# Reordering the RMS chains of a streaming-attention and SwiGLU kernel on one core: block pairs, an order by hand on VectorE, and two copies that change their engine

## The chip, the cores and the metric

The kernel runs on one core of a Trainium2 chip. The metric is the time of one execution on the device, in microseconds (us). A core has several engines, each with its own instruction queue: TensorE (PE in the profile, its weight loads PEld), VectorE (DVE), ScalarE (ACT), GpSimd (POOL) and SyncE (SP, which here only issues DMAs). They meet at semaphores. Matmul results land in PSUM, here eight banks of 128 x 512 fp32; everything else lies in SBUF.

## What is computed

```python
# attention: q, k, v are (4, 8, 768, 64); n_sink 4, window 128
scores = scale * np.matmul(q, k.transpose(0, 1, 3, 2))
keep = is_sink | in_window          # keys 0..3, and the last 128 up to the query
scores = np.where(keep, scores, -1000000000.0)
a = softmax(scores)
attn = np.matmul(a, v)
# the heads side by side: x is (3072, 512)
rms = np.sqrt(np.mean(x * x, axis=-1, keepdims=True) + 1e-06)
xn = x / rms * rms_g
g = xn @ w_gate                     # 512 -> 1536
silu = g * (1.0 / (1.0 + np.exp(-g)))
out = (silu * (xn @ w_val)) @ w_out # 1536 -> 512
```

Inputs and output are fp32; the kernel works in bf16 with fp32 sums.

## The kernel before, in words

The 3072 tokens are 24 blocks of 128 (6 in each of 4 batches). Four blocks make a group of 512 tokens (`GB`, `GN`); there are 6 groups. The feed-forward of group G runs on TensorE while the attention of the blocks of group G+1 and G+2 is fitted in between.

*Attention of block g.* `unit_t`/`unit_t1` transpose q and k on TensorE into PSUM (`pqk`) and copy them out (`qkT`, L257, L279); from block 14 on, except at a batch's start, SP does it by DMA transposes. `unit_s` makes the scores (`pT`, L411), ScalarE their exponentials (`et`, L420), and `mask` zeroes what lies outside the window, on VectorE for the early blocks (L386), else on GpSimd (L388, L393). `unit_attend` multiplies with v: `unit_sink_av` (L444) opens two banks `pv`, `unit_av` (L458, L462) adds to them, VectorE divides by the sum (`rden` L494, `x` L499), and ScalarE squares with an accumulate (`sq`, L510).

*RMS chain.* `unit_rms(gs)` turns the sums of squares of the blocks in `gs` into reciprocal roots by seven small VectorE instructions (`m` L527 and `y` L533 to L555), a few columns wide, whatever the number of blocks. `unit_xr(g)` scales the block (L573, on VectorE; L569 for block 0, L567 on ScalarE for block 1). `unit_x(g)` transposes the result on TensorE (`pxt`, L596) and copies it to `xnt` (ScalarE L603). From block 12 on `unit_xr` issues an SP DMA transpose in place of all that. `GROUP` says which blocks share a chain: (0,1), (2,3), (4,5), (6), (7), then four at a time.

*Feed-forward.* `parts_f` gives a gate part and a value part per slice of 128 columns of the 1536: `pg` matmuls, ScalarE's tanh `th` (L636); `pvl` matmuls, VectorE's `p` (L641) and `hT` (L649). In groups 1 to 5 that makes 24 parts of four matmuls each. Group 0 is done in two halves of 256 tokens with two slices a part, `fa` then `fb`, 12 parts each. `parts_o` adds 12 output parts (`po` L664, three per block); ScalarE copies the result (`osb`, L671) and SP stores it.

*Order.* `run(parts, slots)` walks the parts; a slot (s, unit) is emitted ahead of part s. The lists of slots are: one for the first half, inline; `FIRST` for the second half and group 0's output; and for later groups what `step` gives, plus the RMS chain of the next group's four blocks: `unit_rms` at part 22, `unit_xr` at 25 and 26, `unit_x` at 27 to 30. For blocks 3, 5, 6 and 7 `unit_av` itself emits the chain. The program order is the engine's order on PE, SP and Pool (`MANUAL`). On VectorE and ScalarE the framework's scheduler orders the instructions, except in the prologue, up to `masks` (L746), where all engines follow the program (`MANUAL_ALL`).

*PSUM.* All accumulators share one pool of eight banks (tag `b1`). A new tile waits until the last reader of its bank is done; that reader is an engine's instruction some eight tiles back, so a late `hT` or `et` holds up a matmul that has nothing else to do with it.

*Weights.* `w_gate` and `w_val` come in six chunks each, `w_out` in two, on GpSimd's DMA queue between the loads of q, k and v, during the prologue and the first half.

Of the kernel before, what the change touches and what calls it, by code (L numbers as in the profile page):

```python
# [28 lines left out]
def kernel(  # L29
# [13 lines left out]
    nc = tc.nc  # L43
# [8 lines left out]
    NB = B * NT  # L52
# [120 lines left out]
    def unit_g():  # L173

        pt = psum.tile([P, 512], FP32, name="pgt", tag="b1")
        for kt in range(KTN):
            nc.tensor.matmul(
                out=pt[:, kt:kt + 1], lhsT=raw[2][0:1, kt * P:(kt + 1) * P],
                rhs=gb[0:1, 0:1], start=True, stop=True, skip_group_check=True,
            )  # L180
        ps = psum.tile([P, 512], FP32, name="pgb", tag="b1")
        nc.tensor.matmul(
            out=ps, lhsT=gb[0:1, 0:P], rhs=raw[2][0:1, :], start=True, stop=True,
        )
        nc.vector.tensor_copy(out=gb, in_=ps)
        nc.scalar.copy(out=gt, in_=pt[:, 0:KTN])

    def unit_cast(i):
        tl = ld.tile([P, H, D], BF16, name=("qs", "ks")[i])
# [209 lines left out]
    def unit_s(g):  # L399

        b, t = divmod(g, NT)
        nq = 2 if t + 1 < NT else 1
        w = nq * P
        per = 512 // w
        nb = HP // per
        banks = [[bank() for hi in range(2)] for u in range(nb)]
        for hp in range(HP):
            u, j = divmod(hp, per)
            for hi in range(2):
                pr = slice(hi * D, (hi + 1) * D)  # L410
                nc.tensor.matmul(  # L411
                    out=banks[u][hi][:, j * w:(j + 1) * w],
                    lhsT=QKT[b][pr, 1, hp, t * P:(t + 1) * P],
                    rhs=QKT[b][pr, 0, hp, t * P:t * P + w],
                    start=True, stop=True,
                )
        for u in range(nb):
            et = epool.tile([P, 2, per, nq, P], BF16, name="et")
            for hi in range(2):
                nc.scalar.activation(  # L420
                    out=et[:, hi].rearrange("p j n c -> p (j n c)"), in_=banks[u][hi],
                    func=ACT.Exp, scale=inv_sqrt_d,
                )

            def masked(u, et, his):
                for hi in his:
                    for j in range(per):
                        for n in range(nq):
                            E[(g, 2 * (u * per + j) + hi, n)] = et[:, hi, j, n, :]
                e = et if len(his) == 2 else et[:, his[0]:his[0] + 1]  # L430
                mask(e.rearrange("p i j n c -> p (i j) n c"), g, nq)

            for his in [(0, 1)] if nq == 2 else [(0,), (1,)]:
                masked(u, et, his)

    PVB = {}

# [12 lines left out]
    def unit_av(g, u):  # L450
        b, t = divmod(g, NT)

        pv = PVB.pop((g, u)) if t >= 2 else psum.tile(
            [P, 512], FP32, name="pv", tag="b1")
        for i, h in enumerate(range(H)[heads_of(g, u)]):
            dest = pv[:, i * VW:(i + 1) * VW]
            if t >= 1:
                nc.tensor.matmul(  # L458
                    out=dest, lhsT=E[(g - 1, h, 1)], rhs=V16[b][:, t - 1, h, :],
                    start=(t == 1), stop=False, skip_group_check=True,  # L460
                )
            nc.tensor.matmul(  # L462
                out=dest, lhsT=E[(g, h, 0)], rhs=V16[b][:, t, h, :],
                start=(t == 0), stop=True, skip_group_check=True,
            )
        if u == 0:
            X16[g] = xpool.tile([P, H, D], BF16, name="x16", bufs=7)
        pvv = pv[:, 0:HW].rearrange("p (h c) -> p h c", c=VW)
        if g < 2:
            PV[(g, u)] = pvv  # L470
        else:
            unit_norm(g, u, pvv)
            unit_sq(g, u)
        if u == 1 and g in (3, 5, 6, 7):
            unit_rms(GROUP[g])
            for i in GROUP[g]:
                unit_xr(i)
# [37 lines left out]
    Y = {}  # L515
    GROUP = {}
    for gs in [(0, 1), (2, 3), (4, 5), (6,), (7,)] + [
            tuple(range(g, g + GB)) for g in range(2 * GB, NB, GB)]:
        for g in gs:
            GROUP[g] = gs  # L520

# [64 lines left out]
    def unit_x(g):  # L586
        if g >= DMA_X_FROM:
            return
        G, tb = divmod(g, GB)
        xr = XR.pop(g)  # L590
        n = KTN // 2 if g < 2 else KTN
        for k0 in range(0, KTN, n):
            ps = psum.tile([P, 512], FP32, name="pxt", tag="b1").bitcast(BF16)
            for i in range(n):
                kt = k0 + i
                nc.tensor.transpose(  # L596
                    out=ps[:, i * P:(i + 1) * P], in_=xr[:, kt * P:(kt + 1) * P],
                    identity=ident,
                )
            dest = XNT[G][:, k0:k0 + n, tb * P:(tb + 1) * P]  # L600
            src = ps[:, 0:n * P].rearrange("p (k c) -> p k c", c=P)
            if g >= 2:
                nc.scalar.copy(out=dest, in_=src)  # L603
            elif k0 > 0:
                nc.vector.tensor_tensor(
                    out=dest, in0=src,
                    in1=gt[:, k0:k0 + n].unsqueeze(2).to_broadcast((P, n, P)),
                    op=ALU.mult,
                )
            else:  # L610
                for i in range(n):
                    nc.scalar.mul(dest[:, i, :], src[:, i, :], gt[:, k0 + i:k0 + i + 1])
# [13 lines left out]
                )  # L626
        return ps

    def parts_f(G, fts, cols):
        st = {}  # L630
        n = len(fts)

        def gate():
            st["pg"] = mms("pg", wg, G, fts, cols)
            st["th"] = spool.tile([P, 512], BF16, name="th")
            nc.scalar.activation(out=st["th"], in_=st["pg"], func=ACT.Tanh, scale=0.5)  # L636

        def val():
            pvl = mms("pvl", wv, G, fts, cols)
            p1 = spool.tile([P, 512], BF16, name="p1")  # L640
            nc.vector.scalar_tensor_tensor(  # L641
                out=p1, in0=st["th"], scalar=1.0, in1=st["pg"],
                op0=ALU.add, op1=ALU.mult,
            )
            key = (G, fts[0] // 2)
            if key not in HT:
                HT[key] = hpool.tile([P, 2, GN], BF16, name="hT")
            i = fts[0] % 2
            nc.vector.tensor_tensor(  # L649
                out=HT[key][:, i:i + n, cols],  # L650
                in0=p1.rearrange("p (n c) -> p n c", n=n),
                in1=pvl.rearrange("p (n c) -> p n c", n=n), op=ALU.mult,
            )

        return [gate, val]
# [55 lines left out]
    with tc.manual_schedule(engines=MANUAL_ALL):  # L711
# [56 lines left out]
        (15, lambda: unit_sink(1)),  # L768
        (17, lambda: unit_s(7)),
        (17, lambda: unit_attend(6)),  # L770
        (17, lambda: unit_x(4)),
        (18, lambda: unit_x(5)),
        (19, lambda: unit_t(9)),
        (20, lambda: unit_attend(7)),
        (22, lambda: unit_x(6)),
# [3 lines left out]
        (24, lambda: unit_x(7)),  # L779
    ]  # L780

    with tc.manual_schedule(engines=MANUAL):

        fa, fb = [], []
        for ft in range(0, FA, 2):
            fa += parts_f(0, (ft, ft + 1), slice(0, GN // 2))
            fb += parts_f(0, (ft, ft + 1), slice(GN // 2, GN))
        run(fa, [
            (1, lambda: unit_bias(1, 1)),
            (1, lambda: unit_sp(1, 1)),  # L790
            (1, lambda: unit_sink(0)),
            (2, lambda: unit_t1(3, 0)),
            (3, lambda: unit_s(2)),
            (3, lambda: unit_t1(3, 1)),
            (4, lambda: unit_sink_scores(0, 2)),
            (4, lambda: unit_bias(3, 0)),
            (4, lambda: unit_sp(3, 0)),
# [1 line left out]
            (5, lambda: unit_attend(3)),  # L799
            (11, lambda: unit_x(2)),  # L800
        ])
        for g in range(2 * GB + 2, 2 * GB + 6):
            FIRST.append((3 * g - 28, lambda g=g: unit_load(g)))
        for G in range(NG):
            if G == 0:
                parts, slots = fb, FIRST
            else:
                parts, slots = [], []
                for ft in range(FTN):
                    parts += parts_f(G, (ft,), slice(0, GN))  # L810
                g0, n = (9, 5) if G == 1 else (4 * G + 6, 4)
                for g in range(g0, min(g0 + n, NB + 1)):
                    slots += step(g, AT[G > 1][g - g0])
                if G + 2 <= NG:
                    gs = GROUP[GB * (G + 1)]
                    slots.append((22, lambda gs=gs: unit_rms(gs)))
                    for i, g in enumerate(gs):
                        slots.append((25 + i // 2, lambda g=g: unit_xr(g)))
                        slots.append((27 + i, lambda g=g: unit_x(g)))
            for tb in range(GB):  # L820
                parts += parts_o(G, tb)
            run(parts, slots)
# [33 lines left out]
```

## Time and profile before

| | |
|---|---|
| six runs | 258.53, 259.94, 257.18, 256.47, 258.65, 256.91 us |
| median | 257.85 us (256.47 to 259.94) |
| the profiled execution | 258.53 us, its span 256.8 us |
| mean granted TensorE clock in it | 0.992 |
| DVE, ACT, POOL busy | 161.1, 144.1, 102.9 us |

The profile is of one execution. Its span runs from the first instruction to the last. A line of a timeline gives start, duration, engine, line, operation, tiles (out<-in), and how many instructions it joins; in brackets the idle time of that engine just before and what ended it. A line of waits gives the engine and its instruction, what it waited for, then the total in us, how often, and the longest. Busy time of PE is modelled from pipelined matmuls.

How the stages lie in time: prologue to 17.66 us (first `pg`); group 0's first half to 36.58; its second half and output to group 1's first `pg` at 70.79; the four-block RMS chains at about 101, 137 and 174 us, near the end of a group's gate and value parts.

### The profile page before, as it was taken

Reading aid. Unit: us, or ns where it says so; the run is one execution under the profiler, and the core shown is the slowest. Engines: PE = TensorE matmul, PEld = TensorE weight load, DVE = VectorE, ACT = ScalarE, POOL = GpSimd, SP = SyncE. Lnnn points to the kernel's source line nnn. Section 1 sums busy time; section 2 is a strip of 40 time slices with the busy share of each in tenths; the row PEclk is TensorE's granted clock in tenths of the full one; section 3 lists DMA queues with packets and bytes.
Section 4 is the critical chain, followed back from the end, with each engine's and each line's share of the span. In section 5 each row is a group of like instructions: output and inputs, shape, how many; then the busy total and the mean of one; then the engine's idle time right before and its main releaser. Section 6 shows DMA issues by size and latency. Waiting matters only on the chain.

```text
span 256.8 us, 4881 instructions
## 1 busy us (share of the span) xinstructions
PE 243.0 (95%) x1813; PEld 128.8 (50%) x1838; DVE 161.1 (63%) x375; ACT 144.1 (56%) x327; POOL 102.9 (40%) x141
## 2 busy tenths in 40 slices
PE   8999969999699998999998999999999999999993
PEld 2646857855345553544444444544444444444441
DVE  4656766978338779417779338689148795287700
ACT  2659546889957775864773464773474441323221
POOL 8977586584249999572330100330331000000000
PEclk9999999999979999999999999999999999999999
DMA  9999999999319999999301555001520003400022
GB/s 129 145 173 194 184 165 187 174 155 176 90 41 79 143 152 151 96 141 189 40 3 20 143 146 102 3 3 22 149 78 0 3 0 80 165 3 0 1 82 82
DMA packets 102585, 24.96 MB, mean 97 GB/s; under 512 B 91809, under 2 KB 99489, under 8 KB 102562
## 3 DMA queue, kind: packets, MB, share of 16 engines
q0 software_dynamic: 80704, 13.90, 72.8%
q1 hardware_dynamic: 20818, 10.49, 17.0%
q10 hardware_dynamic: 1040, 0.26, 0.5%
q8 instruction: 14, 0.23, 0.4%
q14 instruction: 9, 0.07, 0.1%
HBM read 28.31 MB, written 6.29 MB: 135 GB/s over the span
## 4 chain that ended last, share of the span: by engine, by line
PE 83%; DVE 8%; ACT 5%; issue 2%; ACTq 0%; DVEq 0%
PE pg L623 23%; PE pvl L623 23%; PE po L664 19%; PE pT L411 4%; PE pv L458 2%; PE pqk L245 2%; PE pv L462 2%; PE pw L332 2%; DVE hT L649 2%; ACT et L420 2%; DVE xr L573 1%; DVE p L641 1%; PE pT L342 1%; PE pT L357 1%; PE pv L444 1%
## 5 line engine op out<-in xcount | busy, mean ns | idle before, releaser
L623 PE MATMUL pg<-xnt,wg 128*128 128x512 bf16 (+1 forms) x324 | 73.5, 347 | 3.6 <-ACT xnt L603 2.8
L623 PE MATMUL pvl<-xnt,wv 128*128 128x512 bf16 (+1 forms) x333 | 74.4, 351 | 0.1
L641 DVE SCALAR_TENSOR_TENSOR p<-th,pg 128x512 bf16<-128x512 bf16 x72 | 49.2, 684 | 35.1 <-ACT th L636 34.9
L636 ACT ACTIVATE th<-pg 128x512 bf16<-128x512 f32 x72 | 43.2, 602 | 42.8 <-PE pg L623 42.6
L664 PE MATMUL po<-wo,hT 128*128 128x512 bf16 x279 | 64.8, 379 | 1.7 <-DVE hT L649 1.2
L649 DVE TENSOR_TENSOR hT<-p,pvl 128x512 bf16<-128x512 bf16 x72 | 49.5, 687 | 7.4 <-PE pvl L623 1.3
L388 POOL TENSOR_SCALAR_AFFINE_SELECT et<-et 128x512 bf16<-128x512 bf16 x28 | 17.7, 640 | 82.8 <-ACT et L420 75.7
L623 PEld LDWEIGHTS <-wv 128*128 128x128 bf16 x336 | 32.6, 98 | 29.4 <-issue 0.3
L623 PEld LDWEIGHTS <-wg 128*128 128x128 bf16 x336 | 31.4, 98 | 28.4 <-issue 3.7
L664 PEld LDWEIGHTS <-hT 128*128 128x128 bf16 x288 | 27.5, 98 | 32.9 <-DVE hT L649 2.2
L420 ACT ACTIVATE et<-pT 128x512 bf16<-128x512 f32 x76 | 39.5, 606 | 5.5 <-PE pT L411 5.5
L671 ACT ACTIVATE osb<-po 128x512 f32<-128x512 f32 x24 | 14.4, 601 | 39.5 <-PE po L664 39.5
L494 DVE RECIPROCAL rden<-pv 128x4 f32<-128x4 f32 x48 | 7.8, 174 | 26.9 <-PE pv L462 26.5
L121 POOL DMA_DIRECT2D v<-in_v_dram x24 | 21.8, 909 | 3.8 <-DMA wo<-in_moe_w_out_dram 2.2
L108 POOL DMA_DIRECT2D qs<-in_q_dram x23 | 20.9, 911 | 4.7 <-DMA wo<-in_moe_w_out_dram 2.9
L510 ACT ACTIVATE sq<-x 128x256 bf16<-128x256 bf16 x48 | 20.3, 428 | 4.4 <-DVE x L499 4.1
L108 POOL DMA_DIRECT2D ks<-in_k_dram x23 | 20.8, 906 | 2.3 <-DMA wv<-in_moe_w_val_dram 1.2
L499 DVE TENSOR_TENSOR x<-pv,rden 128x256 bf16<-128x256 f32 x48 | 19.9, 422 | 1.0
L573 DVE SCALAR_TENSOR_TENSOR xr<-x,y,gb 128x512 bf16<-128x512 bf16 x22 | 15.6, 747 | 0.2
L393 POOL TENSOR_SCALAR_AFFINE_SELECT et<-et 128x512 bf16<-128x512 bf16 x22 | 14.0, 636 | 0.0
L462 PE MATMUL pv<-v,et 128*128 128x65 bf16 x168 | 13.0, 196 | 0.0
L411 PE MATMUL pT<-qkT 64*128 64x256 bf16 (+1 forms) x168 | 12.6, 268 | 0.0
(78 smaller groups left out, 193.5 us busy)
## 6 DMA issues: line engine op xcount, KB each, us to landing
out_dram<-osb SPq DMA_DIRECT2D x24, 256.0 KB, 2.2
v<-in_v_dram POOLq DMA_DIRECT2D x24, 128.0 KB, 6.9
qs<-in_q_dram POOLq DMA_DIRECT2D x23, 128.0 KB, 6.6
ks<-in_k_dram POOLq DMA_DIRECT2D x23, 128.0 KB, 6.7
wg<-in_moe_w_gate_dram POOLq DMA_DIRECT2D x6, 256.0 KB, 8.2
wv<-in_moe_w_val_dram POOLq DMA_DIRECT2D x6, 256.0 KB, 8.3
wo<-in_moe_w_out_dram POOLq DMA_DIRECT2D x2, 768.0 KB, 10.5
osb<-in_k_dram ACTq DMA_DIRECT2D x1, 256.0 KB, 4.6
```

What stands on the lines that cost most here:

```text
L108: nc.gpsimd.dma_start(out=tl, in_=src[b, :, t * P:(t + 1) * P, :].rearrange("h t d -> t h d"),)
L121: nc.gpsimd.dma_start(out=V16[b][:, t, :, 0:D], in_=v[b, :, t * P:(t + 1) * P, :].rearrange("h t d -> t h d"),)
L411: nc.tensor.matmul(out=banks[u][hi][:, j * w:(j + 1) * w], lhsT=QKT[b][pr, 1, hp, t * P:(t + 1) * P], rhs=QKT[b][pr, 0, hp, t * P:t * P + ...
L420: nc.scalar.activation(out=et[:, hi].rearrange("p j n c -> p (j n c)"), in_=banks[u][hi], func=ACT.Exp, scale=inv_sqrt_d,)
L499: nc.vector.tensor_tensor(out=X16[g][:, heads_of(g, u), :], in0=pvv[:, :, 0:D], in1=RDEN.pop((g, u)).unsqueeze(2).to_broadcast((P, 4, D)), ...
L510: nc.scalar.activation(out=sq, in_=xh, func=ACT.Square, scale=MS_SCALE, accum_out=MS[g - i][:, i, u:u + 1],)
L573: nc.vector.scalar_tensor_tensor(out=xr, in0=x16, scalar=y, in1=gb, op0=ALU.mult, op1=ALU.mult,)
L623: nc.tensor.matmul(out=ps[:, i * n:(i + 1) * n], lhsT=w_sb[:, kt, ft * P:(ft + 1) * P], rhs=XNT[G][:, kt, cols], start=(kt == 0), stop=(kt ...
L636: nc.scalar.activation(out=st["th"], in_=st["pg"], func=ACT.Tanh, scale=0.5)
L641: nc.vector.scalar_tensor_tensor(out=p1, in0=st["th"], scalar=1.0, in1=st["pg"], op0=ALU.add, op1=ALU.mult,)
L649: nc.vector.tensor_tensor(out=HT[key][:, i:i + n, cols], in0=p1.rearrange("p (n c) -> p n c", n=n), in1=pvl.rearrange("p (n c) -> p n c", ...
L664: nc.tensor.matmul(out=st["po"], lhsT=HT[(G, ft // 2)][:, ft % 2, tb * P:(tb + 1) * P], rhs=wo[:, ft, :], start=(ft == 0), stop=(ft == FTN ...
```

## The change

It does four things.

1. `unit_g`: the copy of the RMS weight, spread over all partitions (`gb`, 128 x 512, PSUM to SBUF), goes from VectorE to ScalarE, behind `gt`.
2. In group 0's first half VectorE also follows the program order. `parts_f` gets a hook, `between`, that emits units between a value part's `p` and `hT`: the chain of blocks 2 and 3 and xr(2) in the third pair of parts, xr(3) in the fourth. Block 2's masks are held back to slot 4, the k transposes of block 3 go ahead of the scores of block 2, and `unit_av` no longer emits block 3's chain.
3. Block 7's copy from PSUM to `xnt` goes from ScalarE to VectorE; x(4) and x(5) come one slot later.
4. From block 8 on, chains are made for pairs of blocks. While group 1 runs, the pair 8, 9 stands at part 11 and the pair 10, 11 at part 25; while groups 2 to 4 run, the next group's pairs stand at 4 and 25. The xr follow one and two parts after the chain, the x five and six.

```diff
-        nc.vector.tensor_copy(out=gb, in_=ps)
         nc.scalar.copy(out=gt, in_=pt[:, 0:KTN])
+        nc.scalar.copy(out=gb, in_=ps)
...
             for his in [(0, 1)] if nq == 2 else [(0,), (1,)]:
-                masked(u, et, his)
+                if g == 2:
+                    HELD.append(lambda u=u, et=et, his=his: masked(u, et, his))
+                else:
+                    masked(u, et, his)
+
+    HELD = []
+
+    def unit_held():
+        while HELD:
+            HELD.pop(0)()
...
-        if u == 1 and g in (3, 5, 6, 7):
+        if u == 1 and g in (5, 6, 7):
...
-            tuple(range(g, g + GB)) for g in range(2 * GB, NB, GB)]:
+            (g, g + 1) for g in range(2 * GB, NB, 2)]:
...
-            if g >= 2:
+            if g == 2 * GB - 1:
+                nc.vector.tensor_copy(out=dest, in_=src)
+            elif g >= 2:
                 nc.scalar.copy(out=dest, in_=src)
...
-    def parts_f(G, fts, cols):
+    def parts_f(G, fts, cols, between=None):
...
+            if between:
+                between()
             key = (G, fts[0] // 2)
...
-        (17, lambda: unit_x(4)),
-        (18, lambda: unit_x(5)),
+        (18, lambda: unit_x(4)),
+        (19, lambda: unit_x(5)),
...
+    BETWEEN = {
+        4: lambda: (unit_rms((2, 3)), unit_xr(2)),
+        6: lambda: unit_xr(3),
+    }
+        fa += parts_f(0, (ft, ft + 1), slice(0, GN // 2), BETWEEN.get(ft))
+    with tc.manual_schedule(engines=MANUAL | {mybir.EngineType.DVE}):
         run(fa, [
...
+            (3, lambda: unit_t1(3, 1)),
             (3, lambda: unit_s(2)),
-            (3, lambda: unit_t1(3, 1)),
+            (4, lambda: unit_held()),
...
-                    gs = GROUP[GB * (G + 1)]
-                    slots.append((22, lambda gs=gs: unit_rms(gs)))
-                    for i, g in enumerate(gs):
-                        slots.append((25 + i // 2, lambda g=g: unit_xr(g)))
-                        slots.append((27 + i, lambda g=g: unit_x(g)))
+                    for i, p in enumerate((11, 25) if G == 1 else (4, 25)):
+                        g = GB * (G + 1) + 2 * i
+                        slots.append((p, lambda g=g: unit_rms((g, g + 1))))
+                        for j in range(2):
+                            slots.append((p + 1 + j, lambda g=g + j: unit_xr(g)))
+                            slots.append((p + 5 + j, lambda g=g + j: unit_x(g)))
```

More of the change, by code (lines that the diff above doesn't have):

```diff
@@ L780 @@
     ]
[L782 to L787, printed above, removed]
+    BETWEEN = {
+        4: lambda: (unit_rms((2, 3)), unit_xr(2)),
+        6: lambda: unit_xr(3),
+    }
+    fa, fb = [], []
+    for ft in range(0, FA, 2):
+        fa += parts_f(0, (ft, ft + 1), slice(0, GN // 2), BETWEEN.get(ft))
+        fb += parts_f(0, (ft, ft + 1), slice(GN // 2, GN))
+    with tc.manual_schedule(engines=MANUAL | {mybir.EngineType.DVE}):
         run(fa, [
@@ L801 @@
         ])
+    with tc.manual_schedule(engines=MANUAL):
         for g in range(2 * GB + 2, 2 * GB + 6):
```

## Prediction

> **What bounds the kernel now.** I read the engines' shares first, then the waits of TensorE, then the stretches around each wait.
>
> ```profile
> PE 243.0 (95%) x1813; PEld 128.8 (50%) x1838; DVE 161.1 (63%) x375; ACT 144.1 (56%) x327; POOL 102.9 (40%) x141
> ```
> ```profile
> PE pg L623 <- ACT xnt L603: 2.8, 2, 2.2
> PE pxt L596 <- DVE xr L573: 2.3, 2, 1.6
> PE pw L332 <- DVE idle L99: 1.3, 1, 1.3
> PE po L664 <- DVE hT L649: 1.2, 2, 0.9
> PE pxt L596 <- DVE xr L569: 0.5, 1, 0.5
> ```
>
> TensorE bounds it; only its idle 13.8 us, and a clock below full, can be won. The waits (total, times, longest) name the places: all but `pw` are chains that end in an `xr`, an `xnt` or an `hT`, which the change touches. First the three of the first half and the one of block 7:
>
> ```profile
> 14.09 0.69 DVE L185 COPY gb<-pgb 128x512 f32<-128x512 f32 x1 [1.22 <-PE pgb L182]
> 14.70 0.15 DVE L527 SCALAR_TENSOR_TENSOR m<-ms 128x2 f32<-128x2 f32 x1
> 15.94 0.35 DVE L569 TENSOR_SCALAR xr<-x,y 128x512 bf16<-128x512 bf16 x1
> ...
> 30.69 0.15 DVE L527 SCALAR_TENSOR_TENSOR m<-ms 128x2 f32<-128x2 f32 x1
> 33.61 1.41 DVE L573 SCALAR_TENSOR_TENSOR xr<-x,y,gb 128x512 bf16<-128x512 bf16 x2
> 34.41 0.40 PE L596 MATMUL pxt<-ident,xr 128*128 128x128 bf16 x4 [1.56 <-DVE xr L573]
> 36.58 0.60 PE L623 MATMUL pg<-xnt,wg 128*128 128x256 bf16 x4 [0.67 <-ACT xnt L603]
> ...
> 67.70 2.08 ACT L420 ACTIVATE et<-pT 128x512 bf16<-128x512 f32 x4
> 69.61 0.66 ACT L671 ACTIVATE osb<-po 128x512 f32<-128x512 f32 x1
> 70.08 0.65 ACT L603 COPY xnt<-pxt 128x512 bf16<-128x512 bf16 x1
> 70.79 1.02 PE L623 MATMUL pg<-xnt,wg 128*128 128x512 bf16 x4 [2.16 <-ACT xnt L603]
> ```
>
> The last four show ScalarE doing four exponentials and a store copy before block 7's `xnt`, while TensorE stands 2.16 us. Stretches (us, busy of PE, PEld, DVE, ACT, POOL, then the granted clock, DMA share, GB/s):
>
> ```profile
> 68.47:71.88 3.41, 1.25 (x9) 0.54 (x7) 0.00 (x0) 2.30 (x6) 2.40 (x4) 1.00 0.20 77
> 71.88:75.30 3.42, 3.42 (x30) 1.70 (x29) 1.56 (x3) 1.96 (x4) 0.24 (x1) 0.50 0.00 0
> 30.92:34.34 3.42, 1.93 (x18) 1.48 (x16) 3.28 (x11) 1.19 (x2) 2.13 (x4) 1.00 2.43 156
> ```
>
> VectorE is idle in all of the first, and half clock follows it; after the third, with PE busy 1.93, it does not. Last, group 2's end, where the RMS chain of four blocks sits between two FFN pairs:
>
> ```profile
> 134.61 0.69 DVE L641 SCALAR_TENSOR_TENSOR p<-th,pg 128x512 bf16<-128x512 bf16 x1 [1.16 <-ACT th L636]
> 139.40 0.68 DVE L641 SCALAR_TENSOR_TENSOR p<-th,pg 128x512 bf16<-128x512 bf16 x1
> 141.39 0.39 PE L664 MATMUL po<-wo,hT 128*128 128x512 bf16 x1 [0.93 <-DVE hT L649]
> ```
>
> **The change part by part.** The base is the profiled execution, 258.53 us (span 256.8, 1.7 around it), 0.68 above the median 257.85 of the six runs; I put no correction on that.
>
> *gb on ScalarE, start.* VectorE's chain m to xr takes 15.94 − 14.70 = 1.24 and may start at 13.48, when the last square's accumulate ends, so xr(0) begins at 14.75. ScalarE's copy, by `osb<-po` of the same shape (601 ns), ends about 14.7, before xr(1) wants ScalarE. The warm-up matmuls end at 15.88, so the wait of 0.46 goes: −0.5; no gain is the other end, if xr(1) runs late.
>
> *First half by hand.* Holding block 2's masks back brings t1(3,1) and hT forward: the pg after attend(2), at 25.77, comes 0.2 to 0.35 earlier beyond the start's 0.5. What is held is queued before attend(2), which needs it, so at worst that gain is lost. The chain of blocks 2 and 3 waits for the last square's accumulate (30.44). A p at 27.51 (0.65) and an hT at 28.67 (0.69) stood between block 3's norms and now stand behind them, and attend(2) is 0.2 to 0.35 earlier, so that accumulate ends about 1.6 earlier, at 28.85. By the rows' durations (seven small steps 1.24, p 0.68, xr 0.74 each, hT 0.69) the two xr land at 30.8 and 32.7, against x(2) wanted at 32.2 and x(3) at 33.3. Waits 1.56 and 0.67 go; the first pg of the second half, 36.58, comes to 34.3. With the start that is −2.2 (waits in sum 0.46 + 1.56 + 0.67 = 2.7; other end +0.5, nothing won and the masks late). Next in line would be the weights: the last wv chunk landed at 32.02 and is wanted about 32.4, so they do not bind, narrowly.
>
> *x(7) on VectorE.* The transposes end about 68.65 and VectorE is free. Its copy of the same shape, `qkT<-pqk`, takes 420 ns against ScalarE's 598: pg starts at 69.2 for 70.79, −1.6 (ends −1.7 and 0). x(4) and x(5) one slot later stand behind other matmuls and cost nothing; were that cover gone, one xnt, 0.6. The clock: with a gap of 0.55 that stretch would be 84% busy, and 3.42 us at half clock become 1.7: −1.7 (ends −1.7, 0).
>
> The Trainium skill, "VectorE: DVE Perf Modes", Specifications, places VectorE closer to SBUF and ScalarE closer to PSUM, which speaks against this edit. The rows above (420 ns against 598) say the opposite for this shape. By the page at best ScalarE's duration would hold, pg at 69.4, and the sum 254.6.
>
> The Trainium skill, "TensorE: Matmul & The Clock Gate", Why this matters for your kernels, asks only that idle gaps stay under about 3 us. Here half clock followed a wait of 2.16. By the page the half clock would have another source and stay, and the sum would be 256.1.
>
> *Pairs of blocks.* An RMS chain of two and its two xr cost VectorE 2.0: 139.40 − 134.61 = 4.79 with a chain of four and two xr, less two p+hT at 1.40 (119.86 to 121.24). VectorE gets 21 more instructions in all; the second pair stays late, so the early pair is what is new. What is queued behind it are p and hT, which free the accumulator banks of later attention.
> – Group 1, late: the wait of 0.72 at 102.85 (x(8) on xr(8)) goes, −0.72. Early: VectorE has no idle time from 84.65 to 90.6, so 2.0 falls behind p9, and with it the two xnt on ScalarE ahead of th; I take 0.73 for the next block's bank and 0.3 at the tail (ends 0 and 2.0): +1.0.
> – Group 2, early: hT3 moves from 122.03 to 123.27, ends 123.96; sink_av's bank is wanted at 123.35: +0.65 (0 to 2.0). Late: the 0.93 at 141.39 shrinks by 0.15, since p11 waits behind one xr less and one short chain more.
> – Group 3, early: p3 at 160.26 moves to about 161.6; attend(18)'s banks are wanted at 161.0 to 161.15: +0.55 (0 to 2.0). Late: the 0.31 at 177.77 stays.
> – Group 4, early: the banks come free 0.3 to 0.7 before they are wanted: 0 (to 2.0 without that cover).
> SP: the xr transposes of the early pairs (1.2 to 1.3 us each) now pass the q/k transposes and the stores. Those of block 19 were issued at 118.73 and 120.01 and are wanted about 160; some 36 us of slack hide it, and without that the price is one transpose, 1.3. POOL's order does not change.
>
> Sum: −2.2 − 1.6 − 1.7 − 0.72 − 0.15 + 1.03 + 0.65 + 0.55 = −4.1; 258.53 − 4.1 = **254.4 us**, 1.3% under the median. All gains with early pairs free: −2.7 − 1.7 − 1.7 − 0.72 − 0.15 = −7.0, 251.5. All adverse: +0.5 + 4 × 2.0 = 8.5 less 0.87, 266.
>
> **Rivals.**
> – *The clock stays half.* For it: one gap is one observation, and block 7's transposes (0.39 of the 1.25) count in my 84%. Against: PE busy 1.93 of 3.42 kept full clock. 254.4 + 1.7 = 256.1.
> – *The first half gains nothing*, because the order by hand puts VectorE in front of a later wait (held masks ahead of attend(2), xr ahead of hT). For it: VectorE is 3.28 of 3.42 busy there. Against: the chain now ends at 33.61 + 1.41, and 1.8 of it is pulled forward. 254.4 + 2.2 = 256.6. With the first rival too: 258.3.
> – *Slower: the early pairs are exposed in full* at the four places, where the next attention's banks wait for VectorE. For it: VectorE runs back to back at 84.65 to 90.6, and from 117.86 to 124. Against: TensorE needs 1.73 per gate and val, VectorE 1.40, so it catches up 0.33 a pair. 4 × 2.0 = 8.0 in place of my 2.23: 260.2. It decides from about 1.6 per place (all other terms give −6.4).
>
> **How the numbers follow.** Forecast 0.60 (own range 252.3 to 256.3: half of its unknown ends each way), half clock 0.12, first half 0.11, both 0.07, slower 0.10. The range leaves out the slower rival and the forecast's thin lower tail: 252.2 to 258.4. About 1% is what a measurement here can tell from no change: 255.27 to 260.43 around 257.85. Faster is the forecast less the 0.10 of it above 255.27: 0.50. Same is that 0.10, the rivals at 256.1, 256.6 and 258.3, and half of the slower one, whose 260.2 lies at the bound: 0.45. Slower: 0.05.
>
> **What would show it.** No wait of x(0), x(2), x(3) or the second half's first pg over 0.3, and that pg at about 34.3; a VectorE copy behind block 7's transposes with pg about 0.55 later, and no stretch at half clock near 70; no wait of x(8); new waits of 0.5 to 0.8 on banks that p or hT free, at the early pairs of groups 1 to 3; still some 0.8 before group 2's po. Wrong would be a late wv chunk at about 32, a half clock elsewhere, or waits of 1.6 and more at the early pairs.

## The result, and the profile after

The changed kernel takes 255.25 us (median of 19 runs, 254.71 to 256.56), the kernel before 257.72 (40 runs); the ratio is 0.990 with a 95% interval of 0.988 to 0.992. The profiled execution of the changed kernel took 255.38 us, with a span of 253.7 and a mean granted clock of 0.998. Shares of the engines, then what TensorE waited for (total in us, times, longest):

```profile
PE 241.6 (95%) x1813; PEld 128.9 (51%) x1838; DVE 164.1 (65%) x403; ACT 144.3 (57%) x327; POOL 103.0 (41%) x141
```
```profile
PE pw L332 <- DVE idle L99: 1.3, 1, 1.3
PE po L677 <- DVE hT L662: 1.0, 2, 0.6
PE pg L634 <- ACT xnt L614: 0.7, 1, 0.7
PE pT L411 <- ACT qkT L279: 0.7, 1, 0.7
PE pv L453 <- DVE hT L662: 0.5, 1, 0.5
PE pg L634 <- DVE xnt L612: 0.5, 1, 0.5
PE pT L411 <- ACT osb L684: 0.3, 1, 0.3
PE pv L471 <- DVE p L652: 0.3, 1, 0.3
...
PE pv L453 <- DVE p L652: 0.2, 1, 0.2
PE pvl L634 <- DVE hT L662: 0.2, 1, 0.2
```

The long waits for `xr` and the 2.2 for `xnt` are gone. In their place stand several short ones, on `qkT`, `hT` and `p`: accumulator banks and operands that come late from VectorE and ScalarE.

Where the time went is read best from marks: the start of the same instruction in both timelines (a tanh `th` or a store copy `osb` on ScalarE), and how its distance from before moves along the span.

| mark (first or last instruction of its kind) | before, us | after, us | difference | step since the last mark |
|---|---|---|---|---|
| first th, first half | 18.88 | 18.32 | −0.56 | −0.56 |
| first th, second half | 37.65 | 35.49 | −2.16 | −1.60 |
| last osb of group 0 | 69.61 | 67.58 | −2.03 | +0.13 |
| first th of group 1 | 71.85 | 68.19 | −3.66 | −1.63 |
| fourth th of group 1 | 80.33 | 75.12 | −5.20 | −1.54 |
| last osb of group 1 | 112.94 | 107.95 | −4.99 | +0.21 |
| seventh th of group 2 | 126.78 | 122.91 | −3.87 | +1.12 |
| first osb of group 2 | 141.82 | 137.66 | −4.16 | −0.29 |
| first osb of group 3 | 178.20 | 174.59 | −3.61 | +0.55 |
| last osb of group 5 | 252.73 | 249.12 | −3.62 | −0.01 |
| end of the span | 256.82 | 253.68 | −3.14 | +0.48 |

Start, first half, block 7's copy and the clock win 5.3 us; the early pairs give back 1.6. The last step lies behind the last copy, in the landing of the last store: 4.56 from copy to end here, against 3.97 to 4.10 in the other thirteen profiled executions of this study. Nothing in the change asks for it; whether other executions of the changed kernel have it is not recorded.

The first half and block 7 in the changed kernel's timeline:

```profile
28.80 0.16 DVE L536 SCALAR_TENSOR_TENSOR m<-ms 128x2 f32<-128x2 f32 x1
30.05 0.75 DVE L582 SCALAR_TENSOR_TENSOR xr<-x,y,gb 128x512 bf16<-128x512 bf16 x1
...
31.92 0.74 DVE L582 SCALAR_TENSOR_TENSOR xr<-x,y,gb 128x512 bf16<-128x512 bf16 x1
...
34.42 1.03 PE L634 MATMUL pg<-xnt,wg 128*128 128x256 bf16 x8 [0.67 <-ACT xnt L614]
```
```profile
65.67 2.08 ACT L420 ACTIVATE et<-pT 128x512 bf16<-128x512 f32 x4
66.21 0.39 PE L605 MATMUL pxt<-ident,xr 128*128 128x128 bf16 x4
66.64 0.42 DVE L612 COPY xnt<-pxt 128x512 bf16<-128x512 bf16 x1 [1.12 <-PE pxt L605]
67.12 1.04 PE L634 MATMUL pg<-xnt,wg 128*128 128x512 bf16 x4 [0.52 <-DVE xnt L612]
67.58 0.65 ACT L684 ACTIVATE osb<-po 128x512 f32<-128x512 f32 x1
```

The chain begins at 28.80 in place of 30.69 and both `xr` are done at 32.66. VectorE's copy of block 7 starts as the transposes end, beside ScalarE's exponentials.

**Two clusters of the kernel before.** Its 40 times fall into 20 from 256.47 to 257.18 and 20 from 258.26 to 259.94, with none between. The profiled execution before (258.53) is of the upper cluster, and the median lies in the gap between the two. The changed kernel's times show no such gap. The experiments say why.

### The profile page after: what moved, and what is told of

It is laid out like the page before. It is cut to its first block, busy times and chain, and to the rows that moved or that the text cites. A ratio compares the mean times of both kernels' runs of the same rounds, so it can differ in the third digit from the quotient of the medians.

```text
span 253.7 us, 4910 instructions
## 1 busy us (share of the span) xinstructions
PE 241.6 (95%) x1813; PEld 128.9 (51%) x1838; DVE 164.1 (65%) x403; ACT 144.3 (57%) x327; POOL 103.0 (41%) x141
## 4 chain that ended last, share of the span: by engine, by line
PE 75%; DVE 14%; ACT 7%; issue 3%; ACTq 0%; DVEq 0%
PE po L677 21%; PE pg L634 19%; PE pvl L634 18%; DVE hT L662 4%; DVE p L652 4%; PE pT L411 3%; PE pw L332 3%; DVE xr L582 2%; PE pqk L245 2%; PE pv L467 2%; PE pv L471 2%; ACT et L420 2%; ACT sq L519 2%; PE pT L342 1%; DVE et L386 1%
```

## The experiments

The kernel before, run beside each on the same chip, had medians of 257.00, 258.68, 256.83 and 258.44 in the four sets, because the share of its upper cluster differs between them. So times and marks of the kernels are compared, not ratios from different sets. Marks are differences from the profiled execution before. The prologue ahead of all the edits varies between executions: the first `pgb` matmul, whose result `gb` copies, starts at 12.31 to 13.02 us in the fourteen profiled ones. So what a part costs is read between two marks.

The changed kernel has the latest of these starts, 13.02, and its times are longer than the marks allow. x7_on_act and half_by_scheduler are 0.9 above it by the medians and 1.6 by the marks; the two kernels with chains of four again are 2.3 below it by the medians and 1.4 to 1.6 by the marks. So 0.7 to 0.9 us of its median stays unexplained.

### Block 7's copy back on ScalarE, and with TensorE kept busy

```diff
-            if g == 2 * GB - 1:
-                nc.vector.tensor_copy(out=dest, in_=src)
-            elif g >= 2:
+            if g >= 2:
```

> The changed kernel, but block 7's copy from PSUM to xnt goes back to ScalarE. Theory (the copy stands behind four exponentials and a store copy in ScalarE's queue, and the idle TensorE loses its clock): the wait of the first pg of group 1 is again 2.1 to 2.2 in place of 0.52, half clock for 3.4 us follows, the time rises by 1.6 + 1.5 = 3.1, to about 258.4. Rival A (the clock is a matter of where the gap lies against fixed stretches of 3.4 us, and the gap now lies 2 us earlier): the wait comes back without the half clock, +1.6, 256.9. Rival B (the copy's engine matters only by its own duration, 0.58 against 0.42): +0.2, 255.4.

256.18 us (10 runs), 0.9 over the changed kernel; the theory had 258.4 and rival A 256.9. The marks at last osb of group 0, first and fourth th of group 1 are −2.39, −2.39 and −3.94 (changed kernel: −2.03, −3.66, −5.20). So 1.63 of the gain was the copy, by the marks, and rival B is out. The profiled execution shows no half clock although the wait is back, as rival A has it. Two of the ten, 257.29 and 257.95, had mean clocks of 0.989 and 0.993; the other eight 0.996 to 1.0. Stretches of this kernel (columns as in the prediction), first the 3.41 us that end with the wait:

```profile
64.99:68.40 3.41, 1.26 (x10) 0.66 (x8) 0.17 (x1) 3.36 (x8) 1.92 (x4) 1.00 0.37 72
64.42:67.83 3.41, 1.77 (x11) 0.88 (x11) 0.74 (x1) 3.41 (x8) 1.35 (x3) 1.00 0.68 107
67.83:71.25 3.42, 2.85 (x31) 1.47 (x31) 1.06 (x2) 1.72 (x5) 1.05 (x2) 1.00 0.21 77
```

TensorE is idle for 2.15 and busy 1.26 of 3.41, as before the change (1.25 of 3.41), and yet the granted clock behind it is 1.00. The same idle time halves the clock in one execution and not in another.

The kept traces show what differs. In all fourteen the granted clock changes only at whole multiples of 3.413 us from its first change, which lies at 4 to 7 us (19 and 20 of them to the two ends of the half clock of before, 31 and 32 in tail_by_hand, 71 to 73 to the drop at the end of the program). Cut into stretches at these borders, before has its whole wait in one, 68.47:71.88, busy 1.25. In x7_on_act a border at 67.83 falls inside the wait: the second and third lines above, busy 1.77 and 2.85. Over all fourteen traces, the ends of the programs included, every such stretch that was busy for 1.33 us or less was followed by half clock, and every one of 1.55 or more by full clock. So it is the place of the wait against these borders that decides, which is rival A; this is read from the traces, and no run moved the wait on purpose. As an estimate, a wait of 2.16 has the 1.86 to 2.08 us idle that this takes inside one stretch for 41 to 54% of its possible places; 20 of 40 executions of before have the half clock.

The second kernel is the first one with a line added:

```diff
         (24, lambda: unit_x(7)),
+        (24, lambda: unit_warm(9)),
```

> As x7_on_act, with nine matmuls of zeros (128x512, into a bank that nobody reads) behind block 7's transposes, so that TensorE has work for about 1.9 us while it waits for the copy. It adds work that the result does not use. Theory (the half clock comes from TensorE's idle time): pg starts no earlier than in x7_on_act, but at full clock: 1.5 less than x7_on_act, about 256.9. Rival (the half clock comes from elsewhere): the same as x7_on_act, 258.4, or more.

255.95 us (10 runs, 255.63 to 256.42), no execution under 0.997, the same mark at the end as x7_on_act (−2.43 against −2.46). The expected 256.9 was worked out from a half clock that x7_on_act's profiled execution did not have, and from 258.4 for that kernel. Two in ten against none in ten would not decide it; the next kernel does.

### The kernel before, with only that idle time filled

The same line, added to the kernel before; nothing else is changed.

> The kernel before, with nine matmuls of zeros (128x512, into a bank that nobody reads) behind block 7's transposes, and nothing else changed: work that the result does not use, in TensorE's wait of 2.16. The times of the kernel before fall into two clusters, 256.3 to 257.2 at a mean clock of 0.996 to 0.999 and 258.3 to 259.9 at 0.990 to 0.992. Theory (the half clock behind this wait is had by some executions and not by others, about half of them): the filled kernel has the lower cluster alone, median 256.7, no execution under 0.995. Rival (the upper cluster has another source): clusters and median as before.

256.88 us (5 runs, 256.42 to 257.04, clocks 0.998 to 1.0), beside nine executions of the kernel before on the same chip at 258.26 to 259.22 (0.990 to 0.993): ratio 0.993, interval 0.991 to 0.994. The marks are equal to 0.02 up to the fourth th of group 1, −0.12 ahead of it and −1.66 from it to the end: one step of 1.55, at the place of the half clock, and nothing else. The stretches that the prediction showed of before:

```profile
68.47:71.88 3.41, 3.19 (x16) 1.36 (x14) 0.00 (x0) 2.30 (x6) 2.39 (x4) 1.00 0.20 77
71.88:75.30 3.42, 3.37 (x37) 1.78 (x36) 2.41 (x6) 2.83 (x8) 1.23 (x3) 1.00 0.00 0
```

TensorE now works 3.19 of the first and has full clock in the second. The wait for the copy is as long as it was; what went is the half clock behind it. This shows that the upper cluster is this half clock, and that TensorE's idle time is what brings it on.

### The first half ordered by the scheduler again

```diff
-                if g == 2:
+                if g < 0:
...
-        if u == 1 and g in (5, 6, 7):
+        if u == 1 and g in (3, 5, 6, 7):
...
-        4: lambda: (unit_rms((2, 3)), unit_xr(2)),
-        6: lambda: unit_xr(3),
...
-            (3, lambda: unit_t1(3, 1)),
             (3, lambda: unit_s(2)),
-            (4, lambda: unit_held()),
+            (3, lambda: unit_t1(3, 1)),
...
-    with tc.manual_schedule(engines=MANUAL | {mybir.EngineType.DVE}):
+    with tc.manual_schedule(engines=MANUAL):
```

> The changed kernel, but the first token half as before: VectorE ordered by the scheduler, chain of blocks 2 and 3 behind block 3's attention, masks not held, scores of block 2 ahead of the k transposes of block 3. gb stays on ScalarE. Theory: the wait of x(2) is back at about 1.6 less what the start gives, the second half begins 1.6 later, 256.9. Rival (what the half wins is lost again in group 0's second half, because ScalarE and the loads of later blocks set its end): less than 0.5 slower, 255.3 to 255.7.

256.11 us (10 runs), 0.9 over the changed kernel, where the theory had 1.6. The marks stay at −1.12 from the first half to the second (changed kernel: −0.56 to −2.16): the 1.60 of the first half is shown, with the wait of 1.56 at x(2) back in the trace. The rival is out by the marks: group 0's second half wins none of it back (from −1.12 to −0.74 at the last osb of group 0). One of the ten, 257.85, has a mean clock of 0.993; the wait of 1.56 could be its cause, but there is no trace of it.

### gb back on VectorE

```diff
-        nc.scalar.copy(out=gt, in_=pt[:, 0:KTN])
-        nc.scalar.copy(out=gb, in_=ps)
+        nc.vector.tensor_copy(out=gb, in_=ps)
+        nc.scalar.copy(out=gt, in_=pt[:, 0:KTN])
```

> The changed kernel with the gb copy back on VectorE. Theory: the wait ahead of the first block's transposes is back at 0.46, the first pg of both halves comes 0.3 to 0.5 later, and so does the end: about 255.7. Rival (the start's gain is absorbed, because the first half waits for xr(3) or the weights anyway): 255.3.

255.88 us (4 runs, 255.42 to 256.32). TensorE waits 0.76 ahead of the first `pxt`, the first th is 0.69 later than in the changed kernel, the second half's 0.70, the last osb of group 0 0.56. Nothing of it is absorbed on the way. The edit's worth is best read from the first `pgb` matmul to the first th: 5.29 to 5.32 us in all eleven profiled executions with gb on ScalarE, and 5.93 (before), 6.02 (before_filled) and 6.24 (here) with it on VectorE, so 0.6 to 0.9. In group 1 the profiled execution here loses 0.6 more than the changed kernel's, with a wait of 0.7 for an `hT`; why is not shown.

### Chains of four again in groups 2 to 4

```diff
-            (g, g + 1) for g in range(2 * GB, NB, 2)]:
+            (8, 9), (10, 11)] + [tuple(range(g, g + GB)) for g in range(3 * GB, NB, GB)]:
...
-                    for i, p in enumerate((11, 25) if G == 1 else (4, 25)):
+                    for i, p in enumerate((11, 25)) if G == 1 else ():
...
+                    if G > 1:
+                        gs = GROUP[GB * (G + 1)]
+                        slots.append((22, lambda gs=gs: unit_rms(gs)))
+                        for i, g in enumerate(gs):
+                            slots.append((25 + i // 2, lambda g=g: unit_xr(g)))
```

> The changed kernel, but while groups 2 to 4 run the chain is again of four blocks at part 22 with xr at 25 and 26; group 1 keeps its pairs. Theory (an early pair costs by what it delays in the gate and value stage): the waits at 118.6, 119.4 and 157.5 go, -1.1 and -0.55, the wait of group 2's last hT is back at 0.93, +0.3: about 253.9, faster than the changed kernel by 1.4. Rival (the pairs pay for themselves at the end of each group): 255.3 or slower.

252.99 us (4 runs, 252.65 to 253.35), 2.3 under the changed kernel, where 1.4 was expected. By the marks it is 1.4: the mark stays at −5.30 from the last osb of group 1 to the end of the span, where the changed kernel goes from −4.99 to −3.62. The waits at the early pairs are gone, and the first osb of group 2 again stands behind 0.93:

```profile
PE po L677 <- DVE hT L662: 1.3, 2, 0.9
...
PE pT L411 <- ACT qkT L279: 0.7, 1, 0.7
...
PE pvl L634 <- DVE hT L662: 0.2, 1, 0.2
```

No wait for `p` is left in the list; the last two lines are the early pair of group 1.

So in groups 2 to 4 the pairs cost 1.4 net of the 0.29 that they win before group 2's first osb.

### Pairs in group 1, but late

Against fours_late:

```diff
-                    for i, p in enumerate((11, 25)) if G == 1 else ():
+                    for i, p in enumerate((22, 25)) if G == 1 else ():
```

> As fours_late, and the pairs of group 1 stand at parts 22 and 25 in place of 11 and 25. Theory (the place of the early pair costs, not that it is a pair): the waits of 0.16 and 0.65 in group 1's gate and value stage go, the wait of x(8) does not come back, since xr(8) now follows a chain of its own pair: 1.1 less than fours_late, ratio 0.979 to 0.980 to the kernel before. Rival (the chain of 8 and 9 at part 22 is too late for x(8), as the four-block chain was): a wait of 0.5 to 0.9 before x(8) again, no less than 0.2 off fours_late.

253.58 us (4 runs), 0.6 over fours_late by the medians and 0.4 by the mark at the end (−4.90 against −5.30): a miss of both. The wait at x(8) did not come back, yet group 1 waits longer in its gate and value stage:

```profile
79.81 0.51 DVE L536 SCALAR_TENSOR_TENSOR m<-ms 128x2 f32<-128x2 f32 x1
...
83.01 1.42 DVE L582 SCALAR_TENSOR_TENSOR xr<-x,y,gb 128x512 bf16<-128x512 bf16 x2
...
89.36 1.00 ACT L279 COPY qkT<-pqk 128x1024 bf16<-128x1024 bf16 x1
...
90.41 0.61 PE L411 MATMUL pT<-qkT 64*128 64x256 bf16 x8 [0.98 <-ACT qkT L279]
```

`xr` of blocks 8 and 9 still run at 83.0, where part 11 had them (83.25 in the changed kernel). VectorE is ordered by the scheduler there, and it takes a chain up when the data of its blocks are ready, not when its slot comes. A pair is ready as soon as its two blocks are; the chain of four waits for the fourth. It is the pair that makes the chain early, not the slot number.

### Chains of four in all groups

Change 4 is undone, in group 1 too; changes 1 to 3 stay.

```diff
-            (g, g + 1) for g in range(2 * GB, NB, 2)]:
+            tuple(range(g, g + GB)) for g in range(2 * GB, NB, GB)]:
...
-                    for i, p in enumerate((11, 25) if G == 1 else (4, 25)):
...
+                    gs = GROUP[GB * (G + 1)]
+                    slots.append((22, lambda gs=gs: unit_rms(gs)))
+                    for i, g in enumerate(gs):
+                        slots.append((25 + i // 2, lambda g=g: unit_xr(g)))
+                        slots.append((27 + i, lambda g=g: unit_x(g)))
```

> The changed kernel without its fourth edit: chains of four at part 22, x at 27 to 30, in group 1 too; all other edits stay. Theory (in group 1 the pairs lose by waits of 0.16 and 0.65 in the gate and value stage about what they win at x(8)): those waits go, the wait of 0.72 before x(8) is back, 0.2 less than fours_late at the end of group 1: about 252.8, ratio 0.983. Rival (the pairs of group 1 are worth more, as in pairs_late, where a chain that stood at part 22 cost 0.4 more than at 11): 0.4 more than fours_late, 253.4.

252.94 us (4 runs, 252.41 to 253.14), as the theory has it; the wait before x(8) is back at 0.73. Its mark is −6.01 at the fourth th of group 1 and −6.00 at every mark from the last osb of group 1 on; the changed kernel loses 0.21 in group 1. So in group 1 pairs and fours are nearly equal (0.2), and over all groups change 4 costs the changed kernel 2.3 us by the medians and 1.6 by the marks.

### Three moves

```diff
-        (0, lambda: unit_x(3)),
...
+            (11, lambda: unit_x(3)),
...
-        (24, lambda: unit_x(7)),
+        (23, lambda: unit_x(7)),
```

The first kernel with these moves is pairs_late plus them, and its chains in groups 2 to 4 at parts 26, 28 and 29.

> As pairs_late, and three moves: x(3) right behind x(2) at the end of the first half, x(7) one part earlier, ahead of group 0's last output part, and in groups 2 to 4 the chain at part 26 and xr at 28 and 29. Expected: the waits of 0.67 before the second half and 0.52 before group 1 shrink by 0.3 to 0.5 each, the hT waits of 0.93 and 0.33 stay or shrink, as one xr still stands between p and the last hT: 0.6 to 1.0 less than pairs_late, ratio 0.975 to 0.977.

253.08 us (4 runs), 0.5 under pairs_late, a little less than expected. The chains' later slots changed nothing: the waits for hT stay at 0.93 and 0.33, as the scheduler again puts an `xr` ahead of the last hT. On fours_late the moves alone:

> fours_late with the two moves of best: x(3) behind x(2), x(7) ahead of group 0's last output part. Expected from the two traces: 0.1 and 0.4 to 0.5 less than fours_late, 252.4, ratio 0.9815.

252.57 us (4 runs, 251.78 to 252.75), 0.4 under fours_late (0.5 by the mark at the end, −5.78 against −5.30), a little less than the 0.5 to 0.6 expected.

### VectorE by hand at the end of groups 2 to 4

```diff
-    with tc.manual_schedule(engines=MANUAL):
...
+        if G in (2, 3, 4):
+            with tc.manual_schedule(engines=MANUAL):
+                run(parts[:22], [e for e in slots if e[0] < 22])
+            with tc.manual_schedule(engines=MANUAL | {mybir.EngineType.DVE}):
+                run(parts[22:], [(e[0] - 22, e[1]) for e in slots if e[0] >= 22])
...
```

> As fours_late_moves, and in groups 2 to 4 VectorE follows the program from part 22 on, with the four-block chain at part 24 and xr at 25 and 26, so that p and hT of the last value part go ahead of chain and xr. Theory (the hT waits of 0.93 and 0.33 come from xr that the scheduler puts ahead of the last hT, whatever their slot): both waits go, 1.0 to 1.4 less than fours_late_moves, about 251.2, ratio 0.977. Rival (chain and xr behind hT make block 12's, 16's or 20's xnt late, or the attention that shares VectorE): new waits at the start of the next group of 0.5 and more, and no gain.

257.49 us (5 runs, 256.08 to 258.09). The two waits for hT are gone, as the theory has it, but a new one stands before group 2, from a cause that neither theory nor rival names. First SP's issues of fours_late_moves, then those of tail_by_hand:

```profile
98.36 4.32 SPq L686 DMA_DIRECT2D out_dram<-osb  x2
102.77 1.24 SPq L271 DMA_TRANSPOSE qkT<-qs  x1
```
```profile
96.47 1.19 SPq L271 DMA_TRANSPOSE qkT<-qs  x1
...
105.34 1.04 SPq L686 DMA_DIRECT2D out_dram<-osb  x2
106.44 2.19 SPq L271 DMA_TRANSPOSE qkT<-qs  x1
...
111.02 0.60 ACT L684 ACTIVATE osb<-po 128x512 f32<-128x512 f32 x1 [6.62 <-DMA out_dram<-osb]
111.66 0.58 PE L634 MATMUL pg<-xnt,wg 128*128 128x512 bf16 x1 [3.96 <-ACT osb L684]
```

Here the one block that held SP to the program is split into several, and SP's transposes moved ahead of the stores: the first store of group 1 is issued at 105.34 in place of 98.36. A store copy waits for its buffer, whose store was issued late, and TensorE waits for the copy's bank. Half clock follows in the profiled execution; the mean clocks of all five, 0.983 to 0.993, say the same of the others:

```profile
107.99:111.40 3.41, 0.00 (x0) 0.00 (x0) 0.66 (x3) 0.39 (x1) 0.00 (x0) 1.00 1.68 232
111.40:114.82 3.42, 3.16 (x8) 1.13 (x8) 0.00 (x0) 3.42 (x11) 1.82 (x4) 0.50 1.74 149
```

The last kernel keeps the outer block, so that SP's order is untouched, and has chains of four everywhere (from group 2 on at part 24) and the moves:

```diff
+            if G in (2, 3, 4):
+                run(parts[:22], [e for e in slots if e[0] < 22])
+                with tc.manual_schedule(engines=MANUAL | {mybir.EngineType.DVE}):
+                    run(parts[22:], [(e[0] - 22, e[1]) for e in slots if e[0] >= 22])
```

> fours_everywhere with the two moves (x(3), x(7)) and with VectorE by hand from part 22 on in groups 2 to 4, this time inside the one block that holds SP, GpSimd and TensorE to the program, so that SP's order is that of fours_everywhere. Theory (the 3.96 of tail_by_hand came from SP, whose transposes had gone ahead of the stores when the block was cut; the hT waits come from xr that the scheduler puts ahead of the last hT): waits before group 2 as in fours_everywhere, the hT waits of 0.93 and 0.34 gone, which tail_by_hand's marks put at 1.1 and 0.5, the moves 0.5: 2.0 less than fours_everywhere, ratio 0.976 to 0.978. Rival (VectorE by hand at the tail itself makes the next group late): a wait at the start of group 3 or 4, no less than 0.982.

250.51 us (6 runs, 250.24 to 250.72), against 255.25 for the changed kernel; on its chip the kernel before had 256.25 to 256.46 and 258.33 to 259.16 (ratio 0.971, interval 0.967 to 0.976). That is 2.4 under fours_everywhere by the medians and 2.2 by the marks at the end, for the 2.0 expected; the ratio is under the expected one, as eight of the eleven executions of before are of the upper cluster here. SP's stores are again ahead of its transposes (96.24 and 102.74). What the list of TensorE's waits still has:

```profile
PE pw L332 <- DVE idle L99: 1.3, 1, 1.3
PE pxt L605 <- DVE xr L582: 0.7, 1, 0.7
PE pg L634 <- ACT xnt L623: 0.2, 1, 0.2
PE pT L411 <- ACT osb L684: 0.2, 1, 0.2
```

Its mark steps by 1.1 at the first osb of group 2 and by another 0.5 at that of group 3, where fours_everywhere's stays at −6.00, as expected.

## Why the prediction was right, and where its sizes were off

The forecast was 254.4 and the time 255.25. The mechanisms were right; the sum was 1.0 too large against the profiled execution, most of it from the early pair of group 2 (0.47) and the landing of the last store (0.48). By its steps:

| step | predicted | measured |
|---|---|---|
| start and first half | −2.2 | −2.16 |
| x(7) | −1.6 | −1.63, and again 1.63 when undone |
| clock | −1.7 | −1.54 in this pair of executions |
| group 1 | −0.72 + 1.03 = +0.31 | +0.21 |
| group 2 | +0.65 − 0.15 = +0.50 | +1.12 − 0.29 = +0.83 |
| groups 3 and 4 | +0.55 | +0.55 |
| group 0's second half; last store | 0 | +0.13; +0.48 |
| sum | −4.1 | −3.1 |

- *Start and first half.* Right in size and cause: the chain was put at 28.85 and began at 28.80, the xr were put at 30.8 and 32.7 and ended at 30.80 and 32.66, the second half at 34.3 and came at 34.42. One sign was wrong: no wait of the second half's first pg over 0.3 was to be seen, and 0.67 stayed. The 34.3 had the transposes and the copy of block 3 in it, so the sum did not need that wait to go. The start alone is −0.63 from the first `pgb` to the first th, for −0.5, and the half −1.60, for −1.7.
- *x(7).* Right. ScalarE's copy lasts 0.65 against VectorE's 0.42, but most of the 1.63 is the queue: VectorE could start at 66.64, ScalarE only at 67.70 in x7_on_act, 1.45 after its transposes' end. The Trainium skill, "VectorE: DVE Perf Modes", Specifications, has ScalarE closer to PSUM; here the copy from PSUM to bf16 was the shorter one on VectorE; for the fp32 `gb` it is the other way, 0.69 on VectorE and 0.59 on ScalarE.
- *Clock.* The mechanism was right: idle time of TensorE brings it on, and with 0.52 in place of 2.16 no execution of the changed kernel was below a mean clock of 0.994. What failed is that the prediction took the half clock of the profiled execution for a property of the kernel. It is had by half of the executions of before. It won 1.5 from the upper cluster and nothing from the lower, so between the lower cluster (about 256.8) and 255.25 the change brings only 1.5. The forecast counted from 258.53, and so from the upper cluster; the six times shown already lay in two groups, 256.47 to 257.18 and 258.53 up. The forecast of the time itself does not hang on it: from the lower cluster, without the clock's 1.7, the other terms also lead from 256.8 to 254.4.
- *Group 2.* The term of the early pair was mis-sized: 1.12 for 0.65. Its two waits show 0.17 and 0.53 in brackets, 0.70 in all, while the starts move by 1.12. A wait in brackets is counted from the modelled end of the matmul before, which lies behind the next one's start when they are pipelined, so each wait moves the starts by more than it shows: here 0.33 and 0.79. Likewise 0.93 in brackets was worth 1.1 when tail_by_hand took it away.
- *Group 3.* 0.55 was forecast and 0.55 measured, from a wait of 0.31 in brackets; with bounds of 0 to 2.0 on the term, so close a hit is in part luck.
- *Group 1.* Right in sum: the wait of 0.72 at x(8) went, 0.16 and 0.65 came. The larger one is for `qkT`, ScalarE's copy of an operand, and not for a bank that `p` or `hT` frees, as the prediction had it. Where the early pair falls is decided by when its data are ready (pairs_late), which the prediction did not ask.
- *The slower rival* named the right mechanism at a too high price: the early pairs were exposed at about 0.9 (0.21 net and the 0.72 won at x(8)), 1.1, 0.55 and 0, not at 2.0 each.
- *VectorE's instructions* grew by 28 (375 to 403), four chains of seven, and not by the 21 of the prediction; no term of the sum goes by this count.

## What to carry to other kernels

A part of a change that speeds up its neighbour can hide that it costs: here three edits won 5.3 us by the marks, 3.8 without the half clock, and the fourth took 1.6 back (2.3 by the medians), which only undoing each alone shows. Before a sum is made against one profiled execution, look whether the times lie in clusters, and which cluster it is from. An emission slot binds only the engines that follow the program; for the others, what is ready early runs early.

## What the runs showed of the hardware that was not expected

- A wait of TensorE of 2.16 us (busy 1.25 of 3.41) was followed by 3.42 us at half clock in some executions and not in others: 20 of 40, 9 of 25, 9 of 9, 0 of 8 and 8 of 11 executions of the kernel before are in its upper cluster, and with the wait filled 0 of 5. A wait of 3.96 was followed by it in its trace, and the mean clocks of all five executions are at or under 0.993. In the fourteen traces what chooses is how much of the wait falls into one of the stretches of 3.413 us at whose borders the clock changes: busy for 1.33 or less, half clock follows; for 1.55 or more, it does not. Between the two no trace has a case.
- The Trainium skill, "TensorE: Matmul & The Clock Gate", Why this matters for your kernels, asks for no idle gaps of TensorE over about 3 us. Here a gap of 2.16 was already enough: filling it was worth 1.55 us in the trace.
- Nine matmuls of zeros beside a wait that is there anyway cost nothing (x7_on_act_filled, end mark −2.43 against −2.46).
